# Moving the next tile's scores one step behind the values in two of ten visits, halving the last output block, and adding twelve identity matmuls at the start of a fused attention and FFN kernel

## The chip, the cores and the metric

The kernel runs on one core of a Trainium2 chip. The metric is the device time of one execution in microseconds, the median of several runs. The core's engines run side by side and wait for each other by semaphores: TensorE (PE) multiplies matrices, VectorE (DVE), ScalarE (ACT) and GpSimd (POOL) do the elementwise work, and SyncE (SP) issues most DMAs. Each engine works through its own instructions in their order. PE and ACT have the order in which the code is written; that of DVE is laid down by a scheduler when the program is built, except at the start, where DVE and SP follow the written order too.

## The reference

```python
# 8 batches x 8 heads, 576 tokens, head size 64; x @ w_in @ w_out with d_model 512, d_ff 2048
scores = (q @ k.transpose(0, 1, 3, 2)) / sqrt(64)
rel = pos[:, None] - pos[None, :]
mask_local = (rel >= 0) & (rel < 32)                 # heads 0..3
mask_strided = (rel >= 0) & (pos[None, :] % 32 == pos[:, None] % 32)   # heads 4..7
attn = softmax(where(mask, scores, -1e9))
x = (attn @ v) laid out as [4608 tokens, 512]
h = x @ w_in
out = (0.5 * h * (1 + erf(h / sqrt(2)))) @ w_out     # [4608, 512]
```

## The kernel before, in words

**FFN.** The 4608 tokens are 12 tiles of 384 (`NTILE`, `TT`), the hidden units 16 blocks of 128 (`NF`). That makes 192 steps n of one tile and one block. In a step, `ffn_h(n)` (L614) computes H, 128 x 384, with 12 matmuls (L619 to L621: four chunks of the 512 channels, each in three products, since x and w are split into a high part in reduced precision and the rest, xh and xl). `ffn_g(n)` (L624) applies gelu on ACT (L628), casts the high part gh on ACT (L630), and DVE subtracts it to get gl (L632). `ffn_o(n)` (L647) adds to the tile's output O, three blocks of 128 tokens in three PSUM banks, with nine matmuls of 512 columns (L658 to L660). `ffn_o` runs two steps behind `ffn_h`. When a tile's last step is through, `store(t)` (L662) copies each of the three blocks out of PSUM on ACT (L665) and sends it to memory (L667).

**Strided attention** (heads 4 to 7) runs on DVE alone but for its exps: products of q and k by L494, of the softmax and v by L536, a transpose (L544), in small pieces that the loop spreads over all steps (`run_strided`, L688).

**Local attention** (heads 0 to 3) works in jobs of 128 tokens, three to a tile. `band_job(x)` (L282) has parts: 0 is 32 score matmuls (L297); 1 to 3 the softmax (DVE L311, ACT exps L315, DVE again, with DMAs that lay the result out as a band); 4 is 16 value matmuls (L337); 5 casts xh on ACT (L236), 6 subtracts xl on DVE (L238). The scores of tile t lie in two PSUM banks, S0 and S1, columns i*128 to (i+1)*128 for the tile's job i. The values of jobs 0 and 1 of a tile go into a bank called X_L. Those of job 2 go into the last 128 columns of S0 and S1 *of the next tile* (L332), which its three jobs leave free.

**A step in order.** `step(n)` (L850) calls `visit(n)`, then `ffn_h(n)` and `ffn_g(n)`, then pending splits, then `softmaxes(n)` (parts 5 and 6 of the tile whose values were just made, and parts 1 to 3 that are due), then `run_strided`, then `ffn_o(n - 2)`. A visit comes every 16 steps (`value_at`, L801): at step 16*(t-1)+13 it makes the values of tile t, for t = 2 to 11, and, in all but the last, the scores of tile t+1 (`score_at`, L802) right behind them. Below, the "visit of tile 6" is the one at which the *scores* of tile 6 are made, behind the values of tile 5.

**The start.** The first tile's attention, the split of the weights and the first 16 FFN steps run in an order written out by hand: the table `START`, a list of pieces, each naming a job and advancing it by one part. A letter is a kind of job: L local jobs, A and a, b the strided attention of the first tokens, c a weight split, f an FFN step, u a strided unit, w, q, v, S, B, E, e loads. Before all that, 49 tiny matmuls of zeros (L711) run on PE (`lead_in`).

## Time and profile before

| what | value |
|---|---|
| median of 3 runs | 878.74 us (875.07, 878.97, 878.74) |
| profiled execution | 877.5 us |
| span of that execution, first to last instruction | 875.7 us |
| mean granted clock of TensorE | 0.990 of full speed |
| PE busy | 856.4 us, 98% of the span |
| DVE busy | 706.2 us, 81% |
| ACT busy | 482.7 us, 55% |
| instructions | 19634 |

The profile is one execution; its microseconds count from the span's start. A timeline row gives the start, the duration, the engine, the line, the operation, out<-in, shapes and a count, and in brackets the idle time of the engine just before with what ended it. "S<-qk" is a score matmul, "X_L<-band,vl" and "S<-band,vl" are value matmuls, H and O are FFN matmuls. Rows of the same kind that follow one another are one row; its duration is then from the first start to the last end. A window row gives the busy time of each engine in that stretch and the clock that was granted (PEclk, 1.00 is full speed).

### The profile page before, as it was taken

How to read it: one execution, taken by the hardware profiler on the slowest of the kernel's cores; microseconds unless marked ns; L12 is line 12 of the kernel's file. 1: busy time of each engine (PE TensorE's matmuls, PEld its weight loads, DVE VectorE, ACT ScalarE, POOL GpSimd, SP SyncE). 2: the span in 40 equal slices, each digit the busy share in tenths (PEclk: the TensorE clock that was granted, in tenths of full speed). 3: DMA queues.
4: the chain of work that ended last, by engine and by line, in shares of the span. 5: the costliest groups of instructions: out<-in, count | busy, mean ns of one | idle time of the engine just before them, and what ended most of it. 6: DMA issues, size and time to landing. Idle time of an engine off the chain costs nothing.

```text
span 875.7 us, 19634 instructions
## 1 busy us (share of the span) xinstructions
PE 856.4 (98%) x6082; PEld 771.0 (88%) x6082; DVE 706.2 (81%) x4901; ACT 482.7 (55%) x1001; POOL 17.5 (2%) x89
## 2 busy tenths in 40 slices
PE   5999999999999999999999999999999989999998
PEld 4888898999999999999999899989989979989997
DVE  6998999998989997889999979899799993751111
ACT  7888585566465375357355445556547435443222
POOL 5000100000000000000000000000000000000000
PEclk9799999999999999999999999999999999999999
DMA  9695301320310320310311121131032002000001
GB/s 352 223 380 200 115 24 37 108 76 8 128 47 9 101 97 10 104 44 8 97 50 58 55 76 47 34 122 48 9 101 80 12 30 59 18 6 12 26 1 37
DMA packets 34552, 66.67 MB, mean 76 GB/s; under 512 B 6800, under 2 KB 16528, under 8 KB 34448
## 3 DMA queue, kind: packets, MB, share of 16 engines
q1 hardware_dynamic: 34448, 65.43, 22.1%
q8 instruction: 48, 0.79, 0.4%
q14 instruction: 56, 0.46, 0.2%
HBM read 51.64 MB, written 9.44 MB: 70 GB/s over the span
## 4 chain that ended last, share of the span: by engine, by line
PE 90%; DVE 3%; DMA 3%; ACT 2%; SPq 1%; issue 1%; DVEq 0%; ACTq 0%
PE H L619 15%; PE O L659 14%; PE O L660 14%; PE H L621 14%; PE H L620 14%; PE O L658 14%; PE X_L L337 1%; PE S L297 1%; DMA ws<-in_w_dram 1%; DMA qka<-in_qka_dram 1%; DMA sk<-in_ks_dram 1%; DVE ws L161 1%; SPq L326 1%; PE S L337 1%; DVE w L169 1%
## 5 line engine op out<-in xcount | busy, mean ns | idle before, releaser
L628 ACT ACTIVATE H<-H 128x384 f32<-128x384 f32 x192 | 91.3, 476 | 363.0 <-PE H L621 304.3
L619 PE MATMUL H<-xh,w 128*128 128x384 f32 x768 | 261.6, 341 | 1.5 <-DVE gl L632 1.4
L621 PE MATMUL H<-xh,w 128*128 128x384 f32 x768 | 260.6, 339 | 0.0
L620 PE MATMUL H<-xl,w 128*128 128x384 f32 x768 | 259.4, 338 | 0.4 <-DVE xl L238 0.4
L536 DVE SCALAR_TENSOR_TENSOR acc<-sv,sc,acc 128x64 f32<-128x64 f32 x1158 | 249.5, 275 | 0.7
L660 PE MATMUL O<-w,gl 128*128 128x512 f32 x576 | 228.3, 396 | 0.0
L659 PE MATMUL O<-w,gh 128*128 128x512 f32 x576 | 227.7, 395 | 0.0
L658 PE MATMUL O<-w,gh 128*128 128x512 f32 x576 | 224.4, 390 | 0.0
L494 DVE CUSTOM_DVE_ANT_0 junk<-sq,sk 128x64 f32<-128x64 f32 x1290 | 203.8, 217 | 3.5 <-DMA sk<-in_ks_dram 2.4
L632 DVE TENSOR_TENSOR gl<-H,gh 128x384 fp32r<-128x384 f32 x192 | 105.7, 551 | 106.0 <-ACT gh L630 105.1
L619 PEld LDWEIGHTS H<-xh,w 128*128 128x128 f32 x768 | 145.4, 189 | 11.1 <-DVE gl L632 1.7
L620 PEld LDWEIGHTS H<-xl,w 128*128 128x128 f32 x768 | 145.3, 189 | 8.5 <-DVE xl L238 0.8
L621 PEld LDWEIGHTS H<-xh,w 128*128 128x128 f32 x768 | 145.0, 189 | 0.1
L660 PEld LDWEIGHTS O<-w,gl 128*128 128x128 f32 x576 | 108.1, 188 | 23.7 <-DVE gl L632 0.6
L659 PEld LDWEIGHTS O<-w,gh 128*128 128x128 f32 x576 | 108.1, 188 | 18.2
L658 PEld LDWEIGHTS O<-w,gh 128*128 128x128 f32 x576 | 108.5, 188 | 17.3
L494 DVE DVE_READ_ACCUMULATOR2_ANT sc<- 128x1 f32 x1290 | 103.6, 80 | 0.0
L630 ACT CAST gh<-H 128x384 fp32r<-128x384 f32 x192 | 92.2, 480 | 6.1
L628 ACT ACT_TABLE_LOAD x60 | 77.0, 1283 | 1.0
L504 ACT ACT_TABLE_LOAD x35 | 44.9, 1283 | 0.6
L315 ACT ACTIVATE PT_L<-P_L,nm_L 128x64 f32<-128x64 f32 x132 | 44.2, 337 | 0.3
L315 ACT ACT_TABLE_LOAD x24 | 30.8, 1283 | 0.5
(114 smaller groups left out, 488.7 us busy)
## 6 DMA issues: line engine op xcount, KB each, us to landing
ws<-in_w_dram SPq DMA_DIRECT2D x16, 1023.8 KB, 10.1
qk<-in_qk_dram SPq DMA_DIRECT2D x36, 320.0 KB, 5.0
out_dram<-ob SPq DMA_DIRECT2D x34, 256.0 KB, 2.4
vl<-in_vl_dram SPq DMA_DIRECT2D x36, 192.0 KB, 4.3
sk<-in_ks_dram SPq DMA_DIRECT2D x8, 576.0 KB, 5.5
sv<-in_vs_dram SPq DMA_DIRECT2D x8, 576.0 KB, 3.9
band<-PT_L SPq DMA_DIRECT2D x240, 16.0 KB, 1.8
sq<-in_qs_dram SPq DMA_DIRECT2D x4, 576.0 KB, 4.4
```

The source lines that it names most:

```text
L315: nc.scalar.activation(pv[:, :, h, :], p1[:, h * 2 * QB:(h + 1) * 2 * QB].rearrange("p (c t) -> p c t", c=2), AF.Exp, bias=nm[:, h:h + 1], ...
L494: nc.vector.tensor_tensor_reduce(junk, sq[vi, "q"][:, r0 + r, :], sq[vi, "k"][:, c, :], 1.0, 0.0, ALU.mult, ALU.add, ss[u][:, r, c:c + 1])
L536: nc.vector.scalar_tensor_tensor(acc[:, r, :], sq[vi, "v"][:, c, :], wgt, acc[:, r, :], ALU.mult, ALU.add)
L619: nc.tensor.matmul(hp, w1[f][:, 0, c, :], xh[:, c, :], start=(c == 0), stop=False)
L620: nc.tensor.matmul(hp, w1[f][:, 0, c, :], xl[:, c, :], start=False, stop=False)
L621: nc.tensor.matmul(hp, w1[f][:, 1, c, :], xh[:, c, :], start=False, stop=(c == NC - 1))
L628: nc.scalar.activation(hp, hp, AF.Gelu)
L630: nc.scalar.copy(gh, hp)
L632: nc.vector.tensor_tensor(gl, hp, gh.bitcast(F32), ALU.subtract)
L658: nc.tensor.matmul(o, gh[:, sl], w2[f][:, 0, :], start=(f == 0), stop=False)
L659: nc.tensor.matmul(o, gh[:, sl], w2[f][:, 1, :], start=False, stop=False)
L660: nc.tensor.matmul(o, gl[:, sl], w2[f][:, 0, :], start=False, stop=(f == NF - 1))
```

## The change

Three edits and one list. `LATE = (6, 11)` moves the scores of tiles 6 and 11 (and only theirs) to the step after the one that makes the values of tiles 5 and 10; the banks S0 and S1 of the next tile are still taken at the value step, because the values of the third job go into them. `keep_warm(n)` issues n fp32 matmuls of the identity (128 x 128) by itself repeated to 256 columns into a PSUM tile that local job 1 has used for its transposes; the table has `z9` behind the values of A0 and `z3` between the H matmuls of steps 0 and 1; in exchange the lead-in has 37 matmuls and no longer 49. `store` writes the very last block of 128 tokens as two halves of 256 columns, the first copied by ACT, the second by DVE, each with its own DMAs.

```diff
 START = """
...
-    c0 A0 w5 A0 c1 c0 A0 c0 c1 A0 c3 L5 c1 c3 L2 L5 L1 c2 v5 c1 w6 L4 c3 w4 L1 L2 c2 L1 L2 L4 f0 L5 w7
-    c2 L4 c1 c2 f0 f1 L5 c2 f0 c5 f0 L4 c5 f0 c3 f1 c5 f1 f2 c4 f1 c4 c5 c3 f1 f2 f2 c4 c7 L5 f2 c4 c5
+    c0 A0 z9 w5 A0 c1 c0 A0 c0 c1 A0 c3 L5 c1 c3 L2 L5 L1 c2 v5 c1 w6 L4 c3 w4 L1 L2 c2 L1 L2 L4 f0 L5
+    w7 c2 L4 c1 c2 f0 z3 f1 L5 c2 f0 c5 f0 L4 c5 f0 c3 f1 c5 f1 f2 c4 f1 c4 c5 c3 f1 f2 f2 c4 c7 L5 f2
...
+    spare = []
+
+    def keep_warm(n):
+
+        for _ in range(n):
+            nc.tensor.matmul(spare[0][:, 0:2 * P], ident, ident.unsqueeze(1).to_broadcast([P, 2, P]),
+                             start=True, stop=True)
+
...
         p, pts = buffers(f"L{x}", pn)
+        if x == 1:
+            spare.append(pt)
...
-            nc.scalar.copy(ob, ops_[t][a])
-            for c0, c1, r0 in runs(t, a):
-                nc.sync.dma_start(out[r0:r0 + c1 - c0, :], ob[c0:c1, :])
+
+            halves = 2 if t == NTILE - 1 and a == TT // P - 1 else 1
+            for i in range(halves):
+                cs = slice(i * DM // halves, (i + 1) * DM // halves)
+                if i:
+                    nc.vector.tensor_copy(ob[:, cs], ops_[t][a][:, cs])
+                else:
+                    nc.scalar.copy(ob[:, cs], ops_[t][a][:, cs])
+                for c0, c1, r0 in runs(t, a):
+                    nc.sync.dma_start(out[r0:r0 + c1 - c0, cs], ob[c0:c1, cs])
...
-    for i in range(49):
+    for i in range(37):
...
-            if kind in "wqvSBEe":
+            if kind == "z":
+                keep_warm(int(it[1:]))
+            elif kind in "wqvSBEe":
...
-    FIRST, VISIT = 2, 13
+    FIRST, VISIT, LATE = 2, 13, (6, 11)
     value_at = {ready[t - 1] + VISIT: t for t in range(2, NTILE)}
-    score_at = {ready[1] + FIRST: 2, **{n: t + 1 for n, t in value_at.items()}}
+    score_at = {ready[1] + FIRST: 2, **{n + (t + 1 in LATE): t + 1 for n, t in value_at.items()}}
...
-        if score_at.get(n, 0):
-            banks[score_at[n]] = score_banks(score_at[n])
+        new = t + 1 if t else score_at.get(n, 0)
+        if new and new not in banks:
+            banks[new] = score_banks(new)
```

The lines of the kernel move by the added code: in the changed kernel the scores are L307 (L297 before), the values L347 (L337), H L629 to L631 (L619 to L621), gl L642 (L632), O L668 to L670 (L658 to L660), the strided products L504 and L546 (L494 and L536).

PE, at the visit of tile 11, before: behind the last value matmuls (into S_11_10880, the bank S1 of tile 11) come the scores, and behind all 96 of them the step's H. A name's last number is its buffer's.

```order
L337 MATMUL S_11_10880<-band,vl_9847 64x64 [waits PE_49]
L337 MATMUL S_11_10880<-band,vl_9847 64x64 x3
L297 MATMUL S_11_10879<-qk_9865 32x64
L297 MATMUL S_11_10880<-qk_9865 32x64
...
L297 MATMUL S_11_10880<-qk_9901 32x64
L619 MATMUL H_10960<-xh_9023,w_1260 128x384 [waits DVE_49]
```

The same place in the changed program:

```order
L347 MATMUL S_11_10880<-band,vl_9847 64x64 [waits PE_49]
L347 MATMUL S_11_10880<-band,vl_9847 64x64 x3
L629 MATMUL H_10912<-xh_9023,w_1260 128x384 [waits DVE_49]
...
L670 MATMUL O_2_10257<-w_1222,gl_10784 128x512
L307 MATMUL S_11_10879<-qk_9865 32x64 [waits DVE_49]
L307 MATMUL S_11_10880<-qk_9865 32x64 [waits DVE_49]
L307 MATMUL S_11_10879<-qk_9865 32x64
```

The step's 12 H and nine O matmuls now stand between values and scores, and the first score of each bank waits for DVE. What it waits for are the two xl operations that read the same bank (below). The visit of tile 6 has the same change.

DVE, at the visit of tile 6, in the changed program: from the transpose at the end of a strided unit to the two xl operations that read the banks S0 and S1 of tile 6 (S_6_5581 and S_6_5582). L504 is the strided score product, two rows each; the rows left out are more of the same.

```order
L554 STREAM_TRANSPOSE xs_5908<-acc_5761 128x128 [waits DVE_49]
L504 ISA junk_0_0_6038,sc_5994<-sq_5459,sk_5461 128x64 [waits Pool_49]
...
L504 ISA junk_1_1_6048,sc_5994<-sq_5459,sk_5461 128x64 [waits DVE_49]
L504 ISA sc_5994 128x1
L642 TENSOR_TENSOR gl_5628<-H_5614,gh_5627 128x384 [waits PE_49,Activation_49]
L504 ISA junk_2_1_6050,sc_5994<-sq_5459,sk_5461 128x64 [waits DVE_49]
...
L238 TENSOR_TENSOR xl_4817<-X_L_5583,xh_4816 128x2x128 [waits PE_49,Activation_49]
L238 TENSOR_TENSOR xl_4817<-X_L_5583,xh_4816 128x2x128
L238 TENSOR_TENSOR xl_4817<-S_6_5581,xh_4816 128x128 [waits PE_49,Activation_49]
L238 TENSOR_TENSOR xl_4817<-S_6_5582,xh_4816 128x128 [waits PE_49,Activation_49]
```

Six pairs of L504 stand between the transpose and gl, and four more between gl and the xl operations. Before, it was 23 pairs ahead of gl, then four, and the two xl of the banks were not next to each other.

DVE, at the visit of tile 11, in the changed program, from the second step of a strided softmax (L513) on:

```order
L513 TENSOR_TENSOR sc_11469<-sc_11469,m_11570 128x36 [waits DVE_49]
L546 SCALAR_TENSOR_TENSOR acc_11319<-sv_10030,sc_10676,acc_11319 128x64 [waits DVE_49] x5
L642 TENSOR_TENSOR gl_10926<-H_10912,gh_10925 128x384 [waits PE_49,Activation_49]
L546 SCALAR_TENSOR_TENSOR acc_11319<-sv_10030,sc_10676,acc_11319 128x64 [waits DVE_49] x2
L238 TENSOR_TENSOR xl_10070<-X_L_10881,xh_10069 128x2x128 [waits PE_49,Activation_49]
L238 TENSOR_TENSOR xl_10070<-X_L_10881,xh_10069 128x2x128
L238 TENSOR_TENSOR xl_10070<-S_11_10879,xh_10069 128x128 [waits PE_49,Activation_49]
L238 TENSOR_TENSOR xl_10070<-S_11_10880,xh_10069 128x128 [waits PE_49,Activation_49]
```

Before, 25 of the strided products stood ahead of gl (L536 there) and two between gl and xl; now it is five and two.

## Rows read from the trace of the kernel before

**Rows 1.** The page, part 1: busy time, share of the span, number of instructions.

```profile
PE 856.4 (98%) x6082; PEld 771.0 (88%) x6082; DVE 706.2 (81%) x4901; ACT 482.7 (55%) x1001; POOL 17.5 (2%) x89
```

**Rows 2.** Waits of PE: line, releaser, us in total, times, longest.

```profile
PE S L297 <- issue: 2.9, 1, 2.9
PE A L387 <- DMA qka<-in_qka_dram: 1.8, 1, 1.8
```

**Rows 3.** Timeline of PE at the visit of tile 11.

```profile
711.82 1.15 PE L337 MATMUL X_L<-band,vl 96*64 96x64 f32 x32
...
713.36 1.14 PE L297 MATMUL S<-qk 64*32 64x64 f32 x92
717.44 0.30 PE L297 MATMUL S<-qk 64*32 64x64 f32 x4 [2.94 <-issue]
```

**Rows 4.** Windows of PE: stretch, length, busy (instructions), granted clock, DMA share, GB/s.

```profile
8.50:10.50 2.00, 1.97 (x129) 1.00 0.97 380
...
718.50:720.50 2.00, 2.00 (x8) 0.53 0.03 8
720.50:722.50 2.00, 2.00 (x7) 0.61 0.00 0
722.50:724.50 2.00, 2.00 (x12) 1.00 0.00 0
```

**Rows 5.** Timeline of PE: the starts of the visits before and after.

```profile
641.98 1.15 PE L337 MATMUL X_L<-band,vl 96*64 96x64 f32 x32
...
786.42 1.15 PE L337 MATMUL X_L<-band,vl 96*64 96x64 f32 x32
```

**Rows 6.** The page, part 3: a queue that carries instructions; packets, MB, share.

```profile
q8 instruction: 48, 0.79, 0.4%
```

**Rows 7.** Timeline of PE at the visit of tile 6.

```profile
362.64 1.15 PE L337 MATMUL X_L<-band,vl 96*64 96x64 f32 x32
...
365.29 0.44 PE L619 MATMUL H<-xh,w 128*128 128x384 f32 x1
...
367.50 0.39 PE L658 MATMUL O<-w,gh 128*128 128x512 f32 x1
...
369.58 0.33 PE L619 MATMUL H<-xh,w 128*128 128x384 f32 x1
```

**Rows 8.** Timeline of DVE at the visit of tile 6.

```profile
367.64 0.18 DVE L494 CUSTOM_DVE_ANT_0 junk<-sq,sk 128x64 f32<-128x64 f32 x1
...
370.96 0.55 DVE L632 TENSOR_TENSOR gl<-H,gh 128x384 fp32r<-128x384 f32 x1
...
372.01 0.75 DVE L238 TENSOR_TENSOR xl<-X_L,xh 128x256 fp32r<-128x256 f32 x2
372.68 0.28 DVE L238 TENSOR_TENSOR xl<-S,xh 128x128 fp32r<-128x128 f32 x1
```

**Rows 9.** Timeline of ACT at the visit of tile 6: the casts of S.

```profile
369.11 0.47 ACT L236 CAST xh<-S 128x128 fp32r<-128x128 f32 x2
```

**Rows 10.** Timeline of DVE at the visit of tile 11.

```profile
716.68 4.98 DVE L536 SCALAR_TENSOR_TENSOR acc<-sv,sc,acc 128x64 f32<-128x64 f32 x25
```

**Rows 11.** Timeline of PE at the start; last, the group of the transposes.

```profile
14.81 0.63 PE L414 MATMUL A<-ident,va 128*128 128x128 f32 x4 [1.04 <-DVE va L410]
...
22.86 0.68 PE L297 MATMUL S<-qk 64*32 64x64 f32 x32 [4.50 <-DMA qk<-in_qk_dram]
...
L414 PE MATMUL A<-ident,va 128*128 128x128 f32 x4 | 0.6, 280 | 1.0 <-DVE va L410 1.0
```

**Rows 12.** Windows, 20 to 45 us: the busy sum of each engine over them.

```profile
sum 25.00, PE 21.60 PEld 19.10 DVE 24.76 ACT 22.74 POOL 0.00; mean PE 5.40 PEld 4.77 DVE 6.19 ACT 5.69 POOL 0.00
```

**Rows 13.** Timeline of PE, 81 to 85 us.

```profile
83.88 0.44 PE L619 MATMUL H<-xh,w 128*128 128x384 f32 x1 [1.41 <-DVE gl L632]
```

**Rows 14.** Timeline of ACT: the last copy, and a cast of half its width.

```profile
871.90 0.59 ACT L665 COPY ob<-O 128x512 f32<-128x512 f32 x1 [0.77 <-PE O L660]
...
14.38 0.35 ACT L236 CAST xh<-S_L 128x256 fp32r<-128x256 f32 x1
```

## The prediction

> **What bounds the kernel.** I read the page's engine shares first [rows 1]: TensorE (PE) is busy 98% of the span, VectorE (DVE) 81%, ScalarE (ACT) 55%. So only three things can change the time: PE's own work, PE's clock, and PE's waits. Next, PE's waits [rows 2]: after the start there is one of any size, 2.9 us before a score matmul of L297, with "issue" as its releaser: the trace names no engine and no DMA for it. The other rows there lie in the first 84 us.

> PE's timeline shows where it is [rows 3]. At 711.82 the last visit with scores begins: 48 value matmuls, then 96 score matmuls. After 92 of these PE stands still 2.94 us, then runs the last four. [...] What it costs together follows from the visits' starts [rows 3, 5]: 641.98, 711.82, 786.42. An undisturbed period is 69.84; the one with the pause is 74.60. The excess is 4.76 us: 2.94 pause and 1.82 slow clock (the two windows give 2 x 0.47 + 2 x 0.39 = 1.72).

> Why there? The q8 row [rows 6] has 48 packets of 0.79 MB, 16.4 KB each; PE has 6082 matmuls and as many weight loads [rows 1], 253 instructions a packet, so I take q8 for PE's instructions. A visit issues 144 x 2 = 288 instructions in some 2.7 us (711.82 to the pause), where a normal step spreads 42 over 2.21 + 2.08 us (the H and O stages [rows 7]). A visit can therefore hold two packet ends, and the second comes before its successor has been fetched. That is inferred; the rows show the pause and the packets, not their link.

> **The moved scores.** For tiles 6 and 11 PE now issues the 48 value matmuls, a whole step (H and O), and only then the 96 scores. Counts are unchanged. Two bursts of 96 and 192 instructions, some 4.3 us apart, replace one of 288, so a packet has 4.3 us more to arrive; the pause was 2.94. I take the pause at tile 11 and its slow clock as gone: **-4.76**. (Bounds: 0, if the cause is another; -4.76.) At tile 6 there was nothing to gain: PE runs through there [rows 7].

> The move has a price. The values of a tile's third job lie in the last 128 columns of the same two PSUM banks, S0 and S1, into which the next tile's scores go. The new order has a wait on DVE at the first score of each bank: DVE's two xl operations (L238) that read these values. Before, scores came at once behind the values, and nothing on PE waited for those reads. Behind the waiting score stand all of PE's later H and O matmuls. So I compare when PE arrives with when DVE is through, from rows of before in the new order:
> - Tile 6. PE: 362.64 + 1.54 (values, 713.36 - 711.82 [rows 3]) + 2.21 (H, 365.29 to 367.50) + 2.08 (O, 367.50 to 369.58 [rows 7]) = 368.47. DVE [rows 8]: the score-product pairs of L494 start at 367.64, 23 of them to 370.96, 0.144 each. In the new order six stand ahead of the gl operation: 368.51; gl about 0.5: 369.0; four more pairs: 369.6; xl of X_L 0.67 (372.01 to 372.68): 370.25; xl of S0 and S1, 0.2 to 0.28 each: 370.5 to 370.8. PE waits **+2.1**. ACT is no later than DVE: H now ends 1.1 earlier than at 367.50, and its two xh casts of S ended at 369.58 [rows 9], so at 368.5 now.
> - Tile 11. PE: 711.82 + 1.54 + 2.21 + 2.08 = 717.65. DVE [rows 10]: 25 operations of L536 from 716.68, 0.2 each; now five, to 717.68; gl to 718.2; two more to 718.6; xl of X_L to 719.25; both xl of S to 719.65. PE waits **+2.0**.

> Bounds for each: 0, if DVE is earlier than I read; 2.94, the pause itself, if its order slips by a few operations. H of the next step waits with the scores; gelu's and DVE's operations behind it shift by the same time, and DVE, 81% busy, has the room to make it up.

> Does the clock fall behind a 2 us wait? It did behind 2.94 [rows 3, 4]; behind the wait of 1.8 [rows 2], which ends at about 8.5, it did not: the next window is at 1.00 [rows 4]. 2.0 and 2.1 are nearer to 1.8, so I take nothing; bounds 0 and 1.82 each.

> **The warm-up matmuls.** Twelve fp32 matmuls, identity by 256 columns. The nearest row is four transposes of 128 columns, 0.63 us together, one alone 0.28 [rows 11]: (0.63 - 0.28)/3 = 0.117 for 128 columns, so some 0.23 to 0.47 for 256 (the second if the rate holds for two passes). I take 0.47: nine are 4.2 us. They stand behind A0's values, where PE was idle 4.50 us to 22.86 waiting for qk [rows 11], so they fit. Three more, 1.4 us, stand between the H stages of the first two steps. Twelve of the 49 lead-in matmuls (L711) go, under another wait. What can a warmer PE bring? From 20 to 45 us DVE is busy 24.76 of 25 [rows 12]: PE is the one that waits to be fed until 83.88, when it still waits 1.41 for gl [rows 13]. At most 0.24 can be gained: **-0.2**. Worst case: the matmuls run at half clock and overrun, nine at 0.94 = 8.4 against 4.5: +3.9, if it reaches the end, which that 1.41 wait covers in part.

> **The halved last block.** The last copy is 0.59 [rows 14], now halves on two engines. The order has the second half waiting for ACT, so they run in a row: 0.35 for 256 columns on ACT, twice 0.70, +0.11; half of it leaves earlier and the last transfer is half as big. An extra DMA issue stands behind on SP. **0**, bounds -0.3 (half a copy) and +0.6 (a whole one).

> **The sum.** The profiled execution took 877.5: 877.5 - 4.76 + 2.1 + 2.0 - 0.2 = **876.6**. The median of the three runs, 878.74, lies 1.24 above that execution, and they spread from 875.07 to 878.97, so I go about half that way up: **877.3**. A measurement can tell some 0.5%, 4.4 us, from no change: this is no change.

> **Rivals.**
> 1. *The waits do not come, or are short.* DVE's order is estimated by the rows of before; if DVE runs ahead, its xl are done when PE arrives. Then 877.5 - 4.76 - 0.2 = 872.5, with half of one wait 873.6. For it: DVE has slack, 19% of the span. Against: in both visits the rows put DVE two microseconds late, some ten of its operations.
> 2. *The clock falls behind the new waits.* One mechanism, at the first scores of tiles 6 and 11: 1.82 each, decided by whether a wait is longer than some point between 1.8 (no fall) and 2.94 (fall). 876.6 + 1.82 = 878.4; both, 880.3, slower than before. For it: my waits lie in that gap. Against: they lie at its lower end.
> 3. *The pause stays, and the waits are added.* It moves to another burst, or its cause is not the packet: 877.5 + 4.1 - 0.2 = 881.4, slower; with the clock down behind the waits as well, 885. For it: nothing in the rows links pause and packet. Against: it is the only pause on PE without a named releaser, and it stands in the densest burst.
> [...]
> 4. *The warm-up overruns* at half clock and delays the first steps: up to +3.9, 880.5.

> **Chances.** Forecast 0.52, rival 1 0.17, rival 2 0.18, rival 3 0.08, rival 4 0.05. Faster by over 0.5% (under 874.3) needs rival 1 nearly whole and a low draw: 0.16. Slower by over 0.5% (above 883.1) needs rival 3 with a high draw or the clock, or rival 4 atop another: 0.05. The rest, 0.79, is within 0.5%. The range 873.8 to 881.2 leaves out the lower part of rival 1 (0.1) and the upper parts of 3 and 4 (0.1).

> **What would show it.** No "issue" wait on PE near 714, and the period from the tenth to the eleventh visit back from 74.60 to some 72. Two new PE waits of about 2 us at the first moved scores, released by DVE's xl, at some 368.5 and 720 (later by the first wait): if they are under 0.5, rival 1. The granted clock behind them at 1.00; at half, rival 2. At the start, nine matmuls inside the former 4.50 idle, and PE still waiting for gl near 84. I am wrong if the pause is found again at any visit, or if the sum of PE's waits after 84 us is not near 4.

## The result, and the profile after

The changed kernel takes 880.24 us (median of 22 runs, 876.99 to 884.93); the kernel before, in as many runs beside it, 877.54 (874.61 to 880.53). The ratio is 1.0035, with a 95% interval of 1.0023 to 1.0048: **slower by some 3 us**, where the forecast lay 1.4 us under the median shown before. The profiled execution of the changed kernel took 884.93, the longest of its runs; its span is 883.2, against 875.7 before. So its rows are read stretch by stretch, not by their end. Medians and ratios leave out executions at a low clock throughout (one of 1052.9 us at 0.75 in the kernel with four matmuls behind A0 below, one of the kernel before beside it).

First the page's line of busy times and PE's waits of the changed kernel, against [rows 1, 2]:

```profile
PE 863.7 (98%) x6082; PEld 775.6 (88%) x6082; DVE 707.3 (80%) x4902; ACT 490.2 (56%) x1007; POOL 17.7 (2%) x89
```

```profile
PE S L307 <- DVE xl L238: 3.6, 2, 1.9
PE A L397 <- DMA qka<-in_qka_dram: 3.5, 1, 3.5
PE H L629 <- DVE gl L642: 1.8, 2, 1.2
PE S L307 <- DMA qk<-in_qk_dram: 1.5, 2, 1.3
```

The wait on "issue" of [rows 2] is gone. In its place stand two waits on xl, 3.6 us together: these are the moved scores. The others are the start's (qka, qk) but for the 1.2 on gl, at 243.60. That one follows DVE's wait for a late load of the strided keys, as its timeline shows:

```profile
241.40 0.23 DVE L504 CUSTOM_DVE_ANT_0 junk<-sq,sk 128x64 f32<-128x64 f32 x1 [3.73 <-DMA sk<-in_ks_dram]
```

It is not the moved scores': the 46-lead-in kernel below, with the scores in their old order, has the same 3.73 there. The largest piece of the 7.5 us between the two spans lies earlier still. The loop's first visit (values of tile 2, scores of tile 3) begins 3.98 later; PE's timeline before, then in the changed kernel:

```profile
153.14 1.15 PE L337 MATMUL X_L<-band,vl 96*64 96x64 f32 x32
```

```profile
157.12 1.15 PE L347 MATMUL X_L<-band,vl 96*64 96x64 f32 x32
```

Part of it is a late load: the wait for qka is 3.5 here and was 1.8 before [rows 2]. What the warm-up adds is taken up below. Now PE's timeline of the changed kernel at the two visits, with the start of the next visit behind each (the moved score burst is the row with the bracket), against [rows 3, 5, 7]:

```profile
368.06 1.15 PE L347 MATMUL X_L<-band,vl 96*64 96x64 f32 x32
...
375.94 1.35 PE L307 MATMUL S<-qk 64*32 64x64 f32 x96 [1.88 <-DVE xl L238]
...
441.76 1.15 PE L347 MATMUL X_L<-band,vl 96*64 96x64 f32 x32
...
721.66 1.15 PE L347 MATMUL X_L<-band,vl 96*64 96x64 f32 x32
...
729.36 1.35 PE L307 MATMUL S<-qk 64*32 64x64 f32 x96 [1.70 <-DVE xl L238]
...
793.62 1.15 PE L347 MATMUL X_L<-band,vl 96*64 96x64 f32 x32
```

An undisturbed period between visits is 69.80 to 69.84 in all traces of this case; excesses here are over 69.82. Behind tile 6's visit it is 441.76 - 368.06 = 73.70, 3.88 too long; behind tile 11's 71.96, 2.14 too long. Before, the excesses were 0 and 4.78 (74.60 - 69.82). What PE waited for shows DVE's timeline of the changed kernel at both visits:

```profile
373.89 0.55 DVE L642 TENSOR_TENSOR gl<-H,gh 128x384 fp32r<-128x384 f32 x1
374.94 0.75 DVE L238 TENSOR_TENSOR xl<-X_L,xh 128x256 fp32r<-128x256 f32 x2
375.61 0.48 DVE L238 TENSOR_TENSOR xl<-S,xh 128x128 fp32r<-128x128 f32 x2
...
727.50 0.55 DVE L642 TENSOR_TENSOR gl<-H,gh 128x384 fp32r<-128x384 f32 x1
...
728.36 0.74 DVE L238 TENSOR_TENSOR xl<-X_L,xh 128x256 fp32r<-128x256 f32 x2
729.03 0.47 DVE L238 TENSOR_TENSOR xl<-S,xh 128x128 fp32r<-128x128 f32 x2
```

The xl of the banks end at 376.09 and 729.50; the first scores start 0.15 before that, since the bank S0 is free 0.2 before S1. And the clock, in windows of PE of the changed kernel (columns as in [rows 4]):

```profile
376.00:378.00 2.00, 2.00 (x99) 0.87 0.20 22
378.00:380.00 2.00, 2.00 (x8) 0.50 0.88 317
380.00:382.00 2.00, 2.00 (x9) 0.77 0.40 157
...
732.00:734.00 2.00, 2.00 (x12) 1.00 0.00 0
```

Behind the wait of 1.88 the granted clock fell to 0.50; behind the one of 1.70 it stayed at 1.00. 2 x (0.13 + 0.50 + 0.23) = 1.7 us of the 3.88 are the clock's.

At the start, PE's timeline of the changed kernel, against [rows 11]; L245 is the new warm-up, two passes to a matmul:

```profile
20.69 5.04 PE L245 MATMUL S_L<-ident 128*128 128x256 f32 x18
27.01 0.46 PE L307 MATMUL S<-qk 64*32 64x64 f32 x32 [1.28 <-DMA qk<-in_qk_dram]
```

Nine matmuls took 5.04 us, not 4.2, part of it at half clock (the granted clock was 0.50 from 20.70 to 22.00 and 1.00 from 23.50). The end, against [rows 14], ACT's and DVE's halves of the last copy:

```profile
879.10 0.37 ACT L682 COPY ob<-O 128x256 f32<-128x256 f32 x1 [0.77 <-PE O L670]
879.50 0.42 DVE L680 COPY ob<-O 128x256 f32<-128x256 f32 x1 [4.99 <-ACT ob L682]
```

They run one after the other, 0.82 us where one copy took 0.59.

### The profile page after: what moved, and what is told of

It is laid out like the page before. It is cut to its first block, busy times and chain, and to the rows that moved or that the text cites. A ratio compares the mean times of both kernels' runs of the same rounds, so it can differ in the third digit from the quotient of the medians.

```text
span 883.2 us, 19642 instructions
## 1 busy us (share of the span) xinstructions
PE 863.7 (98%) x6082; PEld 775.6 (88%) x6082; DVE 707.3 (80%) x4902; ACT 490.2 (56%) x1007; POOL 17.7 (2%) x89
## 4 chain that ended last, share of the span: by engine, by line
PE 78%; DVE 10%; DMA 7%; ACT 3%; SPq 1%; issue 1%; ACTq 0%; DVEq 0%
PE H L629 13%; PE H L631 13%; PE H L630 13%; PE O L669 12%; PE O L670 12%; PE O L668 12%; DVE acc L546 4%; DVE junk L504 3%; DMA ws<-in_w_dram 3%; DMA qk<-in_qk_dram 1%; PE S L307 1%; DVE gl L642 1%; DMA qka<-in_qka_dram 1%; DMA sk<-in_ks_dram 1%; PE X_L L347 1%
## 5 line engine op out<-in xcount | busy, mean ns | idle before, releaser
L629 PE MATMUL H<-xh,w 128*128 128x384 f32 x768 | 262.0, 341 | 2.2 <-DVE gl L642 1.8
L631 PE MATMUL H<-xh,w 128*128 128x384 f32 x768 | 260.3, 339 | 0.0
L546 DVE SCALAR_TENSOR_TENSOR acc<-sv,sc,acc 128x64 f32<-128x64 f32 x1158 | 250.1, 275 | 0.8
L670 PE MATMUL O<-w,gl 128*128 128x512 f32 x576 | 228.0, 396 | 0.0
L668 PE MATMUL O<-w,gh 128*128 128x512 f32 x576 | 224.1, 389 | 0.0
L504 DVE CUSTOM_DVE_ANT_0 junk<-sq,sk 128x64 f32<-128x64 f32 x1290 | 204.2, 216 | 4.0 <-DMA sk<-in_ks_dram 4.0
L642 DVE TENSOR_TENSOR gl<-H,gh 128x384 fp32r<-128x384 f32 x192 | 105.6, 550 | 110.8 <-ACT gh L640 109.9
L629 PEld LDWEIGHTS H<-xh,w 128*128 128x128 f32 x768 | 145.2, 189 | 13.3 <-DVE gl L642 3.5
L631 PEld LDWEIGHTS H<-xh,w 128*128 128x128 f32 x768 | 145.2, 189 | 0.1
L670 PEld LDWEIGHTS O<-w,gl 128*128 128x128 f32 x576 | 108.0, 187 | 23.1
L668 PEld LDWEIGHTS O<-w,gh 128*128 128x128 f32 x576 | 108.3, 188 | 17.4
L504 DVE DVE_READ_ACCUMULATOR2_ANT sc<- 128x1 f32 x1290 | 102.7, 80 | 0.0
```

Of the source, the lines that this page charges most:

```text
L504: nc.vector.tensor_tensor_reduce(junk, sq[vi, "q"][:, r0 + r, :], sq[vi, "k"][:, c, :], 1.0, 0.0, ALU.mult, ALU.add, ss[u][:, r, c:c + 1])
L546: nc.vector.scalar_tensor_tensor(acc[:, r, :], sq[vi, "v"][:, c, :], wgt, acc[:, r, :], ALU.mult, ALU.add)
L629: nc.tensor.matmul(hp, w1[f][:, 0, c, :], xh[:, c, :], start=(c == 0), stop=False)
L631: nc.tensor.matmul(hp, w1[f][:, 1, c, :], xh[:, c, :], start=False, stop=(c == NC - 1))
L642: nc.vector.tensor_tensor(gl, hp, gh.bitcast(F32), ALU.subtract)
L668: nc.tensor.matmul(o, gh[:, sl], w2[f][:, 0, :], start=(f == 0), stop=False)
```

## The experiments

Theory A: the cost is the moved scores; they remove a pause that is worth less in a usual execution than in the profiled one, and add two waits. Theory B: the cost is the warm-up at the start. Sixteen kernels ran, each in 12 runs beside the kernel before. The diffs are against the kernel before unless they say otherwise; where they read `LATE`, `keep_warm` or `halves`, these are the lines of the change.

| kernel | median us | ratio to before | 95% interval |
|---|---|---|---|
| before, again (first) | 877.29 | 1.0010 | 0.9992 to 1.0028 |
| before, again (second) | 876.87 | 1.0011 | 0.9996 to 1.0026 |
| changed, again | 879.87 | 1.0038 | 1.0020 to 1.0055 |
| all but the moved scores | 879.39 | 1.0020 | 1.0004 to 1.0036 |
| moved scores alone | 879.59 | 1.0029 | 1.0011 to 1.0048 |
| tile 6's scores alone | 878.50 | 1.0013 | 0.9993 to 1.0033 |
| changed, scores two steps later | 877.81 | 1.0004 | 0.9987 to 1.0021 |
| scores two steps later alone | 877.34 | 1.0013 | 1.0000 to 1.0025 |
| tile 11's two steps later alone (first) | 875.04 | 0.9986 | 0.9969 to 1.0003 |
| tile 11's two steps later alone (second) | 875.48 | 0.9985 | 0.9971 to 0.9999 |
| 46 lead-in matmuls | 879.54 | 1.0022 | 1.0005 to 1.0038 |
| warm-up alone | 877.90 | 1.0023 | 1.0006 to 1.0039 |
| nine behind A0 alone | 879.65 | 1.0041 | 1.0021 to 1.0061 |
| four behind A0 alone | 876.70 | 1.0022 | 1.0000 to 1.0043 |
| three between the H stages alone | 875.92 | 0.9998 | 0.9982 to 1.0014 |
| halved last block alone | 876.46 | 1.0005 | 0.9988 to 1.0023 |

The same program as a kernel of its own came out 0.1% above its twin, twice: ratios between 0.999 and 1.002 say little here, and the profiles have to carry the reading. The kernels ran in several rounds, each with the kernel before beside it, so the ratios are compared and not the medians.

**Taking parts away and adding them alone.** All but the moved scores, from the changed kernel:

```diff
-    FIRST, VISIT, LATE = 2, 13, (6, 11)
+    FIRST, VISIT, LATE = 2, 13, ()
```

> The changed kernel with its scores back behind the values at every visit; warm-up matmuls and halved last block kept. Theory A (the cost is in the moved scores: the two waits of PE on the xl operations, 1.9 and 1.7 us, and the slow clock behind the first, 2.0): within 1 us of the kernel before, with the 2.9 us pause back in the visit of tile 11. Theory B (the cost is at the start: the warm-up matmuls hold the first steps up): 2 to 3 us slower than before.

It lay between: 1.0020. Its pause at tile 11 is there again, but a short one, 1.17 us. The moved scores alone:

```diff
+    FIRST, VISIT, LATE = 2, 13, (6, 11)
...
+    score_at = {ready[1] + FIRST: 2, **{n + (t + 1 in LATE): t + 1 for n, t in value_at.items()}}
```

> The kernel before with the scores of tiles 6 and 11 one step later and nothing else. Theory A: 2 to 3 us slower than before, PE waiting on xl at both visits for 1.5 to 2.2 us each, no issue pause. Theory B: within 1 us of before.

As theory A has it: 1.0029. PE's timeline of this kernel at tile 6, and the windows behind it:

```profile
362.26 1.15 PE L347 MATMUL X_L<-band,vl 96*64 96x64 f32 x32
...
370.17 1.35 PE L307 MATMUL S<-qk 64*32 64x64 f32 x96 [1.90 <-DVE xl L238]
...
434.43 1.15 PE L347 MATMUL X_L<-band,vl 96*64 96x64 f32 x32
```

```profile
370.00:372.00 2.00, 1.83 (x99) 1.00 0.08 11
372.00:374.00 2.00, 2.00 (x13) 1.00 0.89 294
```

The same wait, 1.90, this time without a slow clock: the period is 72.17, 2.35 too long. At tile 11 it waited 1.64. The changed kernel itself, again:

> The changed kernel once more, word for word, for a second profile. Theory: the two waits on xl come again in every execution, 1.6 to 1.9 us each (they are set by the order of DVE), and no issue pause; 2 to 3 us slower than before. Open: whether the clock falls again behind one of them; if it falls always behind the first, the visits' period there is again near 73.7, else near 71.8. Rival: the waits of the first profile were a draw, as its pause was.

```profile
366.04 1.15 PE L347 MATMUL X_L<-band,vl 96*64 96x64 f32 x32
...
373.93 1.35 PE L307 MATMUL S<-qk 64*32 64x64 f32 x96 [1.89 <-DVE xl L238]
...
438.22 1.15 PE L347 MATMUL X_L<-band,vl 96*64 96x64 f32 x32
...
725.25 1.35 PE L307 MATMUL S<-qk 64*32 64x64 f32 x96 [1.70 <-DVE xl L238]
```

The waits are fixed: 1.89 and 1.70 again. The clock stayed up, the period at tile 6 is 72.18. A move where no pause had stood, tile 6 alone:

```diff
+    FIRST, VISIT, LATE = 2, 13, (6,)
```

> The kernel before with the scores of tile 6 alone one step later: a move at a visit in which no pause stood. Theory: pure price of a move, one wait of 1.7 to 1.9 us on xl, with 2.0 more in those executions in which the clock falls; 2 to 3 us slower than before, the pause of tile 11 still there. Rival: the move costs nothing, or only together with the others: under 0.5 us.

Wait 1.89, no fall of the clock, and tile 11's pause there with 2.01. The time, 1.0013, points the same way as the theory, but its interval takes in no change.

**What the pause is, and what it costs.** Three lead-in matmuls fewer:

```diff
-    for i in range(49):
+    for i in range(46):
```

> The kernel before with 46 lead-in matmuls and not 49, that is 12 PE instructions fewer ahead of everything else; no order changes. If the 2.9 us pause comes from the end of an instruction packet falling near the end of the densest burst, the packet ends move 12 instructions later against the program, out of that burst (it lay some 8 before its end): no pause, 4 to 5 us faster. If the pause comes from what PE does there (scores, banks, DMA of qk), it stays in its place and the time is that of before.

The gain did not come, but the cause showed. PE's timeline of this kernel at tile 11:

```profile
719.71 1.17 PE L297 MATMUL S<-qk 64*32 64x64 f32 x96
...
723.54 0.33 PE L621 MATMUL H<-xh,w 128*128 128x384 f32 x1 [2.12 <-issue]
```

The pause is no longer in the scores. It now stands ahead of the third H matmul (L621), that is behind two H matmuls. Before, it stood ahead of the last four score records [rows 3]. Four records and two, each with a weight load, are 12 instructions, and 12 is what was taken away at the very start (three matmuls, two passes, a weight load to each). So the pause keeps its place in the count of PE's instructions and not in the program, as the arrival of an instruction packet would.

The trace also has the packets themselves, as records of the queue q8 [rows 6], and they show the link that the prediction had to infer. The DMA of the kernel before, asked for between 714.90 and 715.90, holds one of them:

```profile
q8 instruction: 1, 0.02, 6.4%
```

By its record it ran from 714.91 to 715.94, 3.09 behind the visit's first value matmul, and PE went on at 717.44, 1.50 after it had landed. The kernel with the three warm-up matmuls alone (below) has no pause at tile 11. Its packet started at 713.85, 1.40 ahead of the visit, here between 713.80 and 714.80:

```profile
q8 instruction: 1, 0.02, 6.0%
```

It landed at 714.81, 2.89 before PE came to the same instruction. All 13 such pauses in the profiles of this study, ten at tile 11 and three at tile 6, end 1.10 to 1.63 us after a packet has landed; where PE passes the same places without a pause, the packet had landed at least 2.4 before. So the pause is a packet that comes too late, and its length is how late. What makes one start 1.4 ahead of a visit and another 3.1 behind it is open.

The count also says why only tiles 6 and 11 are hit. The two places are 2402 matmuls apart, five visits of 480 and two, which is 4804 instructions or 19 packets of 253 [rows 1, 6]. Counted in such steps (an estimate), only the visits of tiles 6 and 11 hold two packet ends, one 11 to 14 matmuls behind their start and one 4 to 6 before their end; the other seven hold one.

I had expected that moving the packet's end out of the burst would be enough. It is not: two matmuls behind the burst the packet had still not come, and at tile 6 the same:

```profile
370.19 0.34 PE L619 MATMUL H<-xh,w 128*128 128x384 f32 x1 [1.41 <-DVE acc L536]
```

The trace puts this wait down to a strided product that H does not read. But it stands five or six records behind the place of the other pauses at tile 6, much as the one at tile 11 does, and a packet landed 1.32 before its end: it is one of the 13. (Two more waits, of 1.18 and 0.91 on gl, are DVE's. So one profile shows why this kernel can be slower, 1.0022, but not that it always is.)

The kernel before, unchanged, as a kernel of its own, twice:

> The kernel before once more, word for word, as a kernel of its own: what two samples of the same program differ by, and whether the 2.9 us pause has the same length in another execution. Both theories: no difference in time (under 0.1%). If the pause is the same in every execution, it is there with 2.9 us and a slow clock behind it; if the first profile was a costly draw, it is shorter.

> The kernel before, word for word, a second time as a kernel of its own: no difference, within 0.7 us, and once more a profile in which the pause of tile 11 has a length of its own, between 1 and 3 us.

PE's timeline of the first, at tile 11's visit and the next one's start, and then a window behind the pause:

```profile
712.72 1.15 PE L337 MATMUL X_L<-band,vl 96*64 96x64 f32 x32
...
717.21 0.30 PE L297 MATMUL S<-qk 64*32 64x64 f32 x4 [1.72 <-issue]
...
786.16 1.15 PE L337 MATMUL X_L<-band,vl 96*64 96x64 f32 x32
```

```profile
718.00:720.00 2.00, 2.00 (x8) 0.51 0.04 8
```

PE's timeline of the second:

```profile
712.68 1.15 PE L337 MATMUL X_L<-band,vl 96*64 96x64 f32 x32
...
718.06 0.32 PE L297 MATMUL S<-qk 64*32 64x64 f32 x4 [2.70 <-issue]
...
786.98 1.15 PE L337 MATMUL X_L<-band,vl 96*64 96x64 f32 x32
```

So the length differs between executions of one program. In ten profiles of kernels with as many PE instructions and tile 11's scores in their old place (the two above, the first profile of the kernel before, and seven kernels of this section) the pause and the excess of the period over 69.82 are:

| kernel | pause us | excess us |
|---|---|---|
| before, first profile | 2.94 | 4.78 |
| before, again (second) | 2.70 | 4.48 |
| nine behind A0 | 2.01 | 3.92 |
| before, again (first) | 1.72 | 3.62 |
| tile 6's scores alone | 2.01 | 2.36 |
| four behind A0 | 1.40 | 1.72 |
| warm-up alone | 1.33 | 1.66 |
| all but the moved scores | 1.17 | 1.51 |
| halved last block | 1.06 | 1.41 |
| three between the H stages | none | 0.00 |

The mean excess is 2.5 us, and the profile that the prediction rested on is the dearest of the ten. The three of the kernel before itself, 3.62 to 4.78, are among its upper four; that they overstate what the pause usually costs is shown by the runs of the next kernels. The excess over the pause is 0.32 to 0.35 where the clock stayed up and 1.78 to 1.91 where it fell.

**Moving without the wait.** The scores two steps behind the values, first in the changed kernel, then alone:

```diff
-    score_at = {ready[1] + FIRST: 2, **{n + (t + 1 in LATE): t + 1 for n, t in value_at.items()}}
+    score_at = {ready[1] + FIRST: 2, **{n + 2 * (t + 1 in LATE): t + 1 for n, t in value_at.items()}}
```

> The changed kernel with the scores of tiles 6 and 11 two steps behind the values and not one. By then DVE's xl operations are done. Theory A: no wait on xl, no pause, some 4 us faster than before (4.8 less what the rest of the change costs). Theory B: 2 us faster than before, since the start still costs 2 to 3. If the moved scores cost something else than the wait (a later softmax, a later band), no faster than the changed kernel.

> The kernel before with the scores of tiles 6 and 11 two steps behind the values, nothing else. If moving them without a wait on xl is worth what the runs so far say (two steps later with the warm-up: 1.35 us under the same kernel without the move): 1 to 2 us faster than before. If the pause costs 4.76 in every execution: 4 to 5 us faster. If the gain is eaten by later softmaxes: no change.

Neither waited for xl, neither paused, and each was about as fast as before (1.0004 and 1.0013): short of theory A's 4 us. Against its own kernel without the move (1.0020) the first gained 0.16%. The second lost some of it again: at the value visit after tile 6's it waited 1.0 us on the band's DMA. That this was because the softmax had come two steps later, too, is likely and not shown. So, tile 11 alone two steps later:

```diff
+    FIRST, VISIT, LATE = 2, 13, (11,)
...
+    score_at = {ready[1] + FIRST: 2, **{n + 2 * (t + 1 in LATE): t + 1 for n, t in value_at.items()}}
```

> The kernel before with the scores of tile 11 alone two steps later: the pause goes, no wait on xl, and tile 6 keeps its order. Theory: faster by what the pause costs in a usual execution, 1.4 to 2.5 us. If the moved scores cost elsewhere (a late band): no change.

> The kernel before with the scores of tile 11 alone two steps later, a second time. Theory: a split of the burst costs 0.6, the pause 1.4 to 4.8 (2.7 in the mean of seven profiles): 2 us faster than before. Rival: the first result was a draw: no change.

PE's timeline of the second at tile 11's visit:

```profile
711.96 1.15 PE L347 MATMUL X_L<-band,vl 96*64 96x64 f32 x32
...
722.08 1.17 PE L307 MATMUL S<-qk 64*32 64x64 f32 x96
...
782.35 1.15 PE L347 MATMUL X_L<-band,vl 96*64 96x64 f32 x32
```

No bracket at the scores, and a period of 70.39: splitting the burst costs 0.57, and neither pause nor wait is left. The medians are 875.04 and 875.48, ratios 0.9986 and 0.9985, the second interval just under 1. It is the fastest kernel of the study, by the ratios 1.2 to 1.3 us under the kernel before, at the edge of what these runs can tell, with its own two medians 0.4 apart. This also prices the pause in usual executions of the kernel before: 1.3 and the 0.57 make 1.8; against the two twins (1.0010 and 1.0011) it is 2.2 and 0.57, 2.8. Either is well under 4.76. The first profile of it also shows a pause at tile 6, where that of before had none:

```profile
367.88 0.31 PE L307 MATMUL S<-qk 64*32 64x64 f32 x6 [0.80 <-issue]
```

**The warm-up.** Alone (with 37 lead-in matmuls), then in parts: nine behind A0 with 40, four there with 45, three between the H stages with 46. The nine's edit stands for all four:

```diff
-    c0 A0 w5 A0 c1
+    c0 A0 z9 w5 A0 c1
...
-    for i in range(49):
+    for i in range(40):
```

> The kernel before with the twelve identity matmuls and 37 lead-in matmuls, nothing else. Theory: the nine run 5 us and more and hold up the scores of job 5, for which DVE waits: 1.5 to 2 us slower than before, with a higher mean clock. Rival: the warm-up is hidden and the last block's halves cost the 1.6 us: no change.

> The kernel before with the nine identity matmuls behind A0 and 40 lead-in matmuls, without the three between the first two steps and without anything else. Theory: nine take 5 us and more and hold up the scores of job 5: the same 1 to 2 us as all twelve. Rival: the three between the first H stages are the cost, or the start does not matter: under 0.5 us.

> The kernel before with four identity matmuls behind A0 (45 lead-in matmuls), nothing else. If the nine cost by running past the arrival of qk: four take some 2.5 us, end inside the old idle time, and the time is that of before within 0.7. If any matmul there costs (by keeping DVE or the banks waiting): 1 us or more slower.

> The kernel before with the three identity matmuls between the H stages of steps 0 and 1 (46 lead-in matmuls), nothing else. If the nine carry the cost: before within 0.7. If the three do, holding up H of step 1 by some 2 us: 1.5 to 2 us slower.

The three cost nothing in the runs, 0.9998. The nine alone came out at 1.0041, but its profile, of an execution of 884.50 in runs with a median of 879.65, has another reason beside: a pause of 2.69 at tile 6 as well, with a slow clock. PE's timeline of that kernel, at the start and at tile 6 with the next visit:

```profile
19.80 5.35 PE L245 MATMUL S_L<-ident 128*128 128x256 f32 x18
25.07 0.45 PE L307 MATMUL S<-qk 64*32 64x64 f32 x32
...
364.10 1.15 PE L347 MATMUL X_L<-band,vl 96*64 96x64 f32 x32
...
369.45 0.31 PE L307 MATMUL S<-qk 64*32 64x64 f32 x5 [2.69 <-issue]
...
438.41 1.15 PE L347 MATMUL X_L<-band,vl 96*64 96x64 f32 x32
```

That visit's excess is 4.49. At the start the scores of L307 follow the warm-up without any wait: the nine last until after qk has come. (In the first profile of the changed kernel qk came so late that 1.28 of waiting was left.) With four there is room again, as PE's timeline of that kernel shows:

```profile
18.46 1.99 PE L245 MATMUL S_L<-ident 128*128 128x256 f32 x8
24.03 0.47 PE L307 MATMUL S<-qk 64*32 64x64 f32 x32 [3.58 <-DMA qk<-in_qk_dram]
```

Yet its ratio, 1.0022, is like that of all twelve (1.0023). So the runs don't show that the overrun carries the cost; with 0.1% between twins, the warm-up costs nothing to 1.5 us, and by the runs the three between the H stages are not the part that does.

The profiles do show the start longer. The loop's first visit begins at 154.2 to 158.2 in the five with all twelve matmuls (156.1 in the mean) and at 152.8 to 155.5 in the ten without any (154.1). But loads that come early or late move this start as well, and in the profile of the three alone, whose runs lost nothing, it is 156.2. A cost of 1 to 2 us at the start fits runs and profiles; how much of it is the warm-up's is not settled.

**The halved last block** alone:

```diff
+            halves = 2 if t == NTILE - 1 and a == TT // P - 1 else 1
...
+                    nc.vector.tensor_copy(ob[:, cs], ops_[t][a][:, cs])
```

> The kernel before with the halved last block alone. Theory: no difference (within 0.4 us either way). Rival: 1.5 us slower, by another copy and DMA in a row at the end.

No difference in time. The profiles are sharper: from the start of the last visit to the span's end the unhalved kernels take 89.2 to 89.3 (875.7 - 786.42 in that of before), the halved ones 89.5 to 89.6 (883.2 - 793.62 in that of the change). It costs 0.3.

## Why the prediction was wrong

**The step that failed is the first term of the sum**, "I take the pause at tile 11 and its slow clock as gone: -4.76" (the slow clock is that of the two windows at 0.53 and 0.61 in [rows 4]). That they go is right: no kernel with the moved scores has a pause there. The size is wrong. It was taken as a constant from one profiled execution, and it changes with how late a packet lands: 0 to 4.78 in ten profiles, 2.5 in the mean, and 1.8 to 2.8 by the runs that lose nothing but this pause. The spread of the three runs shown, 3.9 us from 875.07 to 878.97, was nearly as large as the term, and the prediction did not hold it against a price read from one execution. That the measured 880.24 still lies in its range, 873.8 to 881.2, is owed to the range's width and not to the sum, whose sign was wrong. The packet as the cause, which it inferred, was right.

**The two waits** came as predicted: forecast 2.1 and 2.0, measured 1.88 to 1.90 and 1.64 to 1.70, in every profile, from the same two xl operations. What was missed is small: a period with such a wait is 2.35 and 2.15 too long, some 0.45 more than the wait. Part of it is the second bank: the row of the scores lasts 1.35 instead of 1.17, since its first ones start when S0 is free and the rest wait 0.2 more for S1. And a split of the burst costs 0.57 even without a wait. The move at tile 11 therefore costs about what it saves, and the move at tile 6 saves nothing in most executions: a pause stood there in two of the eleven profiles that leave tile 6 alone and keep the count of PE's instructions.

**The sum with the measured sizes**: -2.5 at tile 11; at tile 6 two pauses in eleven profiles, with excesses of 1.1 (70.96 - 69.82) and 4.5, in the mean -0.5; waits +2.35 + 2.15; the clock behind one of seven waits, 1.5 (3.88 - 2.35) / 7 twice, +0.4; the end +0.3; together +2.2, or +2.9 with 1.8 for the pause. The measured difference is 2.7 between the medians and 3.1 by the ratio. The warm-up's part is what lies between, nothing to 1 us, and is not resolved.

**Rival 2** (the clock falls behind a wait) happened in one of the seven waits. Its rule is refuted: between 1.7 and 2.0 us the length of the wait does not decide it. The clock fell behind the pause of 1.72 and the wait of 1.88, and not behind the waits of 1.89 and 1.90 nor, in the kernel with tile 6's scores alone, behind a pause of 2.01 (excess 2.36). **Rival 1** (no waits) is out by the rows. **Rival 3** (the pause stays) did not occur in the changed kernel.

The link between pause and packet, which the prediction left as inferred, rests on the 12 instructions of the 46-lead-in kernel and on the packets' own times: in this kernel's densest burst a packet that lands late is a wait of up to 2.94 us, and one stood at tile 11 in nine of the ten profiles of the table. Of the nine visits with scores, seven show no pause in any profile with this count of instructions.

**The warm-up**: predicted -0.2, hidden in an idle of 4.50. A matmul took 0.56 to 0.69 (5.04 to 6.17 for nine) and not 0.47; part of them ran at a granted clock of 0.50 (20.70 to 22.00 in the changed kernel's profile). They filled the idle and more. That a higher clock brings nothing was right: in the mean over the runs the granted clock was 0.996 in the kernel with the warm-up alone and 0.992 in the kernel before beside it, and it was no faster. What the matmuls added at the start, 0 to 2 us, lies inside rival 4's bound of 3.9. **The halved block**: predicted 0, measured +0.3.

## What to carry to other kernels

A stall for which the trace names no releaser may have another length in the next execution (here none to 2.94 us); look for it in the records of the queue that carries the instructions, profile the same program several times before its removal is booked as a gain, and compare the runs' spread with its price. Before work is moved away from its neighbour, list who else uses the same PSUM bank: here a bank shared with the values turned an unconditional start into a wait of 1.64 to 1.90 us for another engine. And one step more of distance, only where a pause often stands, came out some 1.3 us faster where the change lost 3.
